# Gated linear attention with an expert layer on one core: a new order of steps, zero products in the head, and the last chunks copied out in halves

## The chip, the cores and the metric

The kernel runs on one core of a Trainium2 chip. The metric is the device time in microseconds (us). The kernel before took 226.56 us as the median of three runs, from 225.03 to 228.58.

## What is computed

```
attention, for each of 4 batches and 8 heads, 768 positions t, head size 48:
    f      = 1 / (1 + exp(-f_logit))
    state  = f[t] * state + outer(k[t], v[t])          # 48 x 48
    y[t]   = q[t] @ state
x = y laid out as 3072 tokens x 384
h = x @ w_in                                            # 384 -> 2048
P = a0 + a1 h + a2 h^2 + a3 h^3
Q = 1 + |b0| |h| + |b1| h^2
out = (P / (Q + 1e-6)) @ w_out                          # 2048 -> 384
```

All inputs and the output are float32; inside, most operands are bfloat16.

## The kernel before

The work is cut into twelve units: unit `n` is one batch and 256 positions (two chunks of 128). Each unit goes through the attention in chunk form and then through the expert layer. The program has no loops over these stages. A string, `ORDER`, lists some 830 steps, each with its unit and its range, and the program emits them in that order. Each engine executes its own steps strictly in the order of the table, and waits at a step until its operands are there, so the table fixes the order on every engine and DMA queue. A trailing `@i` gives the step a new tile in PSUM slot `i`; there are four slots of two banks each, and a new tile waits until the readers of the slot's last tile are done.

The steps of a unit `n`, with the engine in brackets:

- `ld n f|k|q|v`: loads, issued by SP for f, k and q, and by POOL for v (three buffers each). `wi`, `wo`: loads of w_in and w_out in pieces (POOL). `hv 0` is a tiny write that holds w_in's loads back (VectorE). `ab_`, `b1_`: the coefficients.
- `ef`, `ls` (ScalarE): exp of the gates, and log of one plus it. `cs` (TensorE): its cumulative sums. `A n x` (ScalarE): their exponentials. `xa n x` (VectorE): q (x = 0) or k (x = 1) times these.
- `T` (TensorE): transposes; `Te` (VectorE): their copy out of PSUM. `sc`: scores; `mk` (VectorE): scores times mask. `vm`: copies of parts of v (POOL, in unit 0 ScalarE). `sv`, `id` (TensorE): the state's update, `ae` (ScalarE) and `st` (VectorE) its decay. `yb` (TensorE): y; `ye` (ScalarE): its copy out.
- `h n m0 m1` (TensorE): columns m0 to m1 (of 16, each 128 wide) of x @ w_in. `hy` (ScalarE): the copy out; `sa` (ScalarE) or `sq` (VectorE): the square; `ab` (VectorE): the absolute value.
- Q: `u` (TensorE) adds both in PSUM and `ln` (ScalarE) takes the logarithm; or `zd`, an accumulating DMA on POOL's queue, adds them and `lz` (ScalarE) takes the logarithm. `ex` (ScalarE): 1/Q from it.
- P: `p1`, `p2`, `pm` (VectorE), then the sum by `ta` (an accumulating DMA on POOL's queue) or `tv` (VectorE). `gm` (VectorE): P/Q.
- `o n j m0 m1` (TensorE): chunk j's share of the product with w_out. `oe` copies it out (`s` ScalarE, `v` VectorE), `so`, `s0`, `s1` store it (s1 from ScalarE's queue).

In the profile, L200 is a load, L308 `ef`, L313 `ls`, L332 `A`, L337 `xa`, L348 `T`, L356 `Te`, L377 `mk`, L474 `h`, L488 `hy`, L508 `u`, L540 `ex`, L559 `ta`, L525 `zd`, L568 `gm`, L575 `o`, L584 a store, L590 `oe`.

For the last unit, `n` = 11, both chunks' products lie in one tile of one slot (a bank each). The table of before ends with

```
o 11 1 12 16; o 11 0 8 12; oe 11 1 2 v; o 11 0 12 16; s1 11 1 2; s0 11 1 2; oe 11 0 1 s; s1 11 0 1; s0 11 0 1
```

The step `wm` (products of zeros) exists, but the table of before has none.

Of the kernel before, what the change touches and what calls it, by code (L numbers as in the profile page):

```python
# [8 lines left out]
F32 = mybir.dt.float32  # L9
# [10 lines left out]
b1_; cz 3; cb; ld 0 f 2 4; ld 0 f 0 2; ca; cz 0; ld 0 q 2 4; cz 2; ld 0 k 2 4; cz 1; cc; ef 0 2 4  # L20
ld 0 k 0 2; fa 0; ls 0 2 4; ld 0 q 0 2; ef 0 0 2; cs 0 2 4 @0; ls 0 0 2; ld 0 v; A 0 0 2 4
id 0 0 @1; A 0 1 2 4; xa 0 0 2 4; rg; cs 0 0 2 @2; ld 1 f; xa 0 1 2 4; ae 0; A 0 1 0 2; hv 0; ab_
T 0 2 4 @0; wi 0 4; A 0 0 0 2; xa 0 1 0 2; Te 0 2 4; xa 0 0 0 2; sc 0 1 @0; ld 1 k; T 0 0 2 @2
wi 4 8; mk 0 1; vc 0; Te 0 0 2; vm 0 0 s; sv 0; vm 0 1 s; ld 1 v; sc 0 0 @2; st 0 0; ld 1 q; wi 8 16
mk 0 0; id 0 1; st 0 1; yb 0 0 4 @2; ef 1; ld 2 f; fa 1; ls 1; ye 0; cs 1 @1; fb; h 0 0 4 @2; A 1 0
A 1 1; h 0 4 8 @1; hy 0 0 4; xa 1 1; ld 2 k; id 1 0 @2; hy 0 4 8; xa 1 0; ld 2 q; ae 1; sv 1; vm 1 0
vm 1 1; ab 0 0 8; T 1 @1; ld 2 v; sq 0 0 8; Te 1; u 0 0 4 @0; ef 2; ld 3 f; u 0 4 8 @3; st 1 0
ln 0 0 4; p1 0 0 8; id 1 1; sc 1 0 @1; ln 0 4 8; st 1 1; sc 1 1 @0; mk 1 0; ls 2; ex 0 0 8; mk 1 1
id 2 0 @3; ld 3 k; cs 2 @1; pm 0 0 8; yb 1 0 4 @0; A 2 1; wo 8 12; h 0 12 16 @2; p2 0 0 8; ye 1
wo 4 8; xa 2 1; A 2 0; h 1 4 8 @0; wo 0 4; ld 3 q; tv 0 0 8; hy 0 12 16; wo 12 16; h 1 0 4 @1; ae 2  # L30
sa 1 4 8; xa 2 0; ld 4 f; hy 1 4 8; gm 0 0 8; ld 3 v; T 2 @2; hy 1 0 4; vm 2 1; h 0 8 12 @0; Te 2
vm 2 0; sa 1 0 4; sv 2; ab 1 0 8; ef 3; sc 2 0 @1; h 1 12 16 @2; st 2 0; hy 0 8 12; mk 2 0; ls 3
ld 4 k; u 1 0 4 @0; ab 0 8 16; hy 1 12 16; p1 0 8 16; cs 3 @1; ln 1 0 4; sq 0 8 16; h 1 8 12 @2
A 3 0; p2 0 8 16; u 0 12 16 @0; A 3 1; pm 0 8 16; hy 1 8 12; id 2 1; u 0 8 12 @1; ln 0 12 16; st 2 1
sc 2 1 @2; tv 0 8 16; id 3 0 @3; ld 4 q; ln 0 8 12; u 1 4 8 @0; mk 2 1; ae 3; ex 0 8 16
o 0 0 0 4 @1; o 0 0 4 8; p1 1 0 16; yb 2 0 4 @2; ln 1 4 8; o 0 1 0 4; ab 1 8 16; ye 2; xa 3 0
o 0 1 4 8; ex 1 0 8; h 2 0 4 @2; pm 1 0 8; ld 5 f; gm 0 8 16; h 2 4 8 @0; hy 2 0 4; xa 3 1; ef 4
o 0 1 8 12; sq 1 8 16; ld 5 k; o 0 1 12 16; sa 2 4 8; ld 4 v; sv 3; sa 2 0 4; p2 1 0 16; o 0 0 8 12
vm 3 0; ls 4; vm 3 1; ld 5 q; u 1 12 16 @2; st 3 0; ta 1 0 8; hy 2 4 8; pm 1 8 16; o 0 0 12 16
ln 1 12 16; id 3 1; ld 6 f; T 3 @0; st 3 1; ta 1 8 16; ef 5; ab 2 0 8; u 1 8 12 @3; Te 3; oe 0 0 2 s  # L40
zd 2 0 8; h 2 12 16 @2; ln 1 8 12; so 0 0 2; ls 5; sc 3 1 @3; sc 3 0 @0; h 2 8 12 @1; mk 3 1; ld 6 k
ex 1 8 16; ld 5 v; mk 3 0; cs 4 @3; vm 4 1; hy 2 8 12; vm 4 0; cs 5 @0; A 4 0; yb 3 0 4 @1; gm 1 0 8
A 4 1; ye 3; xa 4 0; o 1 0 0 4 @3; hy 2 12 16; o 1 1 0 4; xa 4 1; ld 6 q; h 3 4 8 @1; A 5 0
ab 2 8 16; A 5 1; sq 2 8 16; h 3 0 4 @2; hy 3 4 8; xa 5 0; ef 6; T 4 @0; gm 1 8 16; hy 3 0 4
u 2 12 16 @1; ld 7 f; Te 4; sv 4 @2; ln 2 12 16; id 4 0; ab 3 0 8; sc 4 1 @0; lz 2 0 8; p1 2 0 16
u 2 8 12 @1; o 1 1 4 8; mk 4 1; ln 2 8 12; o 1 1 8 12; o 1 1 12 16; pm 2 8 16; ex 2 0 8; sc 4 0 @1
h 3 12 16 @0; p2 2 0 16; ld 7 k; ae 4; ex 2 8 16; o 1 0 4 8; st 4 0; ta 2 8 16; mk 4 0; id 4 1
o 1 0 8 12; ld 6 v; ld 7 q; o 1 0 12 16; ls 6; xa 5 1; vm 5 0; yb 4 0 4 @1; hy 3 12 16; vm 5 1
st 4 1; pm 2 0 8; ld 8 f; sv 5 @2; oe 1 0 2 s; id 5 0; ef 7; sq 3 0 8; T 5 @3; ta 2 0 8; so 1 0 2
ae 5; ls 7; h 3 8 12 @0; st 5 0; zd 3 0 8; ye 4; Te 5; id 5 1; cs 6 @1; hy 3 8 12; st 5 1  # L50
h 4 4 8 @3; gm 2 8 16; A 6 1; ld 8 k; A 6 0; xa 6 1; h 4 0 4 @0; hy 4 4 8; sq 3 8 16; sc 5 0 @1
sa 4 4 8; h 4 12 16 @2; mk 5 0; hy 4 0 4; ld 8 q; ab 3 8 16; h 4 8 12 @3; vm 6 1; sa 4 0 4; ld 7 v
p1 3 0 16; hy 4 12 16; u 3 12 16 @0; vm 6 0; hy 4 8 12; ab 4 0 8; u 3 8 12 @2; pm 3 8 16; ef 8
sv 6 @3; ln 3 8 12; gm 2 0 8; id 6 0; cs 7 @1; ld 9 f; ae 6; ln 3 12 16; st 6 0; sc 5 1 @2; pm 3 0 8
id 6 1; A 7 1; o 2 0 0 4 @0; ex 3 8 16; o 2 0 4 8; st 6 1; xa 6 0; zd 4 0 8; o 2 0 8 12; o 2 1 0 4
sq 4 8 16; lz 3 0 8; o 2 1 4 8; ab 4 8 16; T 6 @3; mk 5 1; A 7 0; o 2 1 8 12; ld 9 k; o 2 1 12 16
ex 3 0 8; p2 3 0 16; u 4 8 12 @2; xa 7 1; yb 5 0 4 @1; ta 3 0 8; ln 4 8 12; xa 7 0; ta 3 8 16
o 2 0 12 16; ye 5; p1 4 0 16; u 4 12 16 @2; vm 7 1; ld 9 q; ls 8; vm 7 0; h 5 4 8 @1; oe 2 0 2 s
ld 8 v; Te 6; ln 4 12 16; h 5 12 16 @0; pm 4 8 16; sa 5 4 8; so 2 0 2; hy 5 4 8; p2 4 0 16
sc 6 0 @2; cs 8 @3; hy 5 12 16; h 5 0 4 @1; pm 4 0 8; A 8 1; mk 6 0; h 5 8 12 @0; A 8 0; ta 4 0 8  # L60
hy 5 0 4; gm 3 0 8; sc 6 1 @2; sv 7 @3; sa 5 0 4; id 7 0; mk 6 1; ld 10 f; hy 5 8 12; o 3 0 0 4 @1
ta 4 8 16; o 3 1 0 4; gm 3 8 16; ae 7; ef 9; yb 6 0 4 @0; lz 4 0 8; st 7 0; o 3 0 4 8; p1 5 0 16
ld 10 k; o 3 0 8 12; ye 6; ab 5 0 8; o 3 0 12 16; ex 4 8 16; pm 5 0 8; zd 5 0 8; h 6 12 16 @0
xa 8 1; ld 9 v; h 6 8 12 @2; ls 9; ab 5 8 16; vm 8 1; hy 6 12 16; ld 10 q; vm 8 0; sq 5 8 16; id 7 1
o 3 1 4 8; ex 4 0 8; o 3 1 8 12; st 7 1; pm 5 8 16; u 5 8 12 @0; h 6 4 8 @3; hy 6 8 12; p2 5 0 16
ln 5 8 12; h 6 0 4 @2; gm 4 0 8; ta 5 0 8; sa 6 4 8; ab 6 8 16; T 7 @0; hy 6 4 8; ta 5 8 16
gm 4 8 16; o 3 1 12 16; sa 6 0 4; o 4 0 0 4 @3; Te 7; hy 6 0 4; o 4 1 0 4; ld 11 f; ef 10; sq 6 8 16
# [563 lines left out]
```

## Time and profile before

| | us |
|---|---|
| median of three runs | 226.56 (225.03 to 228.58) |
| the profiled execution's own time | 224.93 |
| its span, first to last instruction | 223.2 |
| TensorE busy | 205.2 (92%) |
| VectorE busy | 203.3 (91%) |
| ScalarE busy | 201.1 (90%) |
| GpSimd (POOL) busy | 70.4 (32%) |
| HBM read, written | 25.17 MB, 4.72 MB |

Busy time is what the profiler records between an instruction's start and its end; matmuls overlap, so a busy TensorE isn't one at its peak. A line of the timeline gives start, duration, engine, source line, operation, output and input tiles with their shapes, and in brackets the idle time of the engine before it and what ended that. "PEld" is TensorE's load of weights, "SPq" and "ACTq" are the issues of DMAs by those engines. The chain of work that ended last is followed back from the last instruction, at each step to what released it or to the instruction before it on its engine.

### The profile page before, as it was taken

What the parts mean: (1) busy time and instruction counts of PE and PEld (TensorE: products, weight loads), DVE (VectorE), ACT (ScalarE), POOL (GpSimd) and SP (SyncE); (2) the same over time, 40 slices, a digit from 0 to 9 for tenths busy, and PEclk for the clock granted to TensorE, in tenths of its full rate; (3) what the DMA queues carried; (4) which work ended last, traced back from release to release, by engine and by line L of the source; (5) the groups of instructions that cost most, each with busy time, mean ns of one, the idle gap of its engine ahead of it and who ended that gap; (6) DMA issues with size and microseconds to landing.
All of it is one profiled execution on the core that took longest, in us unless ns stands there. A gap on an engine that the chain in (4) does not pass through costs nothing.

```text
span 223.2 us, 7133 instructions
## 1 busy us (share of the span) xinstructions
PE 205.2 (92%) x3128; PEld 144.0 (65%) x3128; DVE 203.3 (91%) x248; ACT 201.1 (90%) x215; POOL 70.4 (32%) x94
## 2 busy tenths in 40 slices
PE   1786799999999997999999999999999999999991
PEld 1544378566766686567777668678578587785550
DVE  6865999999789997999999999999999999999960
ACT  5645599999999999999999999999999999999960
POOL 3662930021500333107334244041395311341000
PEclk9999999999999999999999999999999999999998
DMA  6999999998999999977999999938869999597434
GB/s 156 225 230 210 237 202 204 193 248 232 170 180 244 243 184 216 260 193 144 171 233 248 209 238 244 213 74 134 171 117 184 207 188 212 112 206 150 94 91 120
DMA packets 61984, 42.33 MB, mean 190 GB/s; under 512 B 51458, under 2 KB 57346, under 8 KB 61954
## 3 DMA queue, kind: packets, MB, share of 16 engines
q0 software_dynamic: 19648, 22.61, 61.6%
q1 hardware_dynamic: 42144, 19.08, 35.0%
q8 instruction: 24, 0.39, 0.6%
q10 hardware_dynamic: 162, 0.20, 0.2%
q14 instruction: 6, 0.05, 0.1%
HBM read 25.17 MB, written 4.72 MB: 134 GB/s over the span
## 4 chain that ended last, share of the span: by engine, by line
PE 62%; ACT 20%; DMA 7%; SPq 4%; issue 3%; DVE 3%
PE op L575 26%; PE hp L474 18%; DMA fn<-in_f_logit_dram 7%; PE u L508 5%; ACT hy L488 4%; PE y L394 4%; ACT lq L516 4%; ACT qi L540 3%; PE tp L348 3%; SPq L200 3%; ACT h L496 3%; ACT A L332 3%; PE sc L369 2%; ACT lsp L313 1%; ACT fn L308 1%
## 5 line engine op out<-in xcount | busy, mean ns | idle before, releaser
L474 PE MATMUL hp<-xT,w_in_sb 128*128 128x256 bf16 x576 | 68.6, 274 | 2.3 <-issue 1.3
L575 PE MATMUL op<-w_out_sb,gall 128*128 128x384 bf16 x384 | 68.7, 326 | 1.1 <-DVE osb L590 0.6
L474 PEld LDWEIGHTS <-w_in_sb 128*128 128x128 bf16 x576 | 55.9, 98 | 12.8 <-issue 3.6
L488 ACT CAST hy<-hp 128x1024 bf16<-128x1024 f32 x48 | 49.5, 1050 | 4.1 <-PE hp L474 4.0
L575 PEld LDWEIGHTS <-gall 128*128 128x128 bf16 x384 | 36.3, 98 | 25.0 <-issue 1.8
L540 ACT ACTIVATE qi<-lq 128x2048 bf16<-128x2048 f32 (+1 forms) x25 | 46.4, 1874 | 0.0
L559 POOL DMA_DIRECT2D gall<-hy x21 | 21.3, 1109 | 64.1 <-PE hp L474 16.4
L377 DVE TENSOR_TENSOR scm<-sc,mask 128x1024 bf16<-128x1024 f32 x24 | 28.7, 1217 | 3.3 <-PE sc L369 3.3
L568 DVE TENSOR_TENSOR gall<-gall,qi 128x2048 bf16<-128x2048 bf16 (+1 forms) x25 | 29.5, 1181 | 0.7 <-ACT qi L540 0.6
L555 DVE TENSOR_TENSOR gall<-gall,h 128x2048 bf16<-128x2048 bf16 (+1 forms) x25 | 29.3, 1177 | 0.0
L388 POOL COPY vmp<-vn 128x128 bf16<-128x128 bf16 x22 | 18.1, 927 | 22.9 <-DMA vn<-in_v_dram 22.9
L525 POOL DMA_DIRECT2D z<-h x12 | 13.2, 1097 | 37.9 <-ACT xT L456 13.4
L516 ACT ACTIVATE lq<-u 128x1024 f32<-128x1024 f32 x24 | 24.5, 1048 | 0.3 <-PE u L508 0.3
L532 ACT ACTIVATE lq<-z 128x2048 f32<-128x2048 bf16 x12 | 23.5, 1956 | 0.0
L492 DVE TENSOR_TENSOR h<-hy 128x2048 bf16<-128x2048 bf16 (+1 forms) x18 | 20.9, 1166 | 0.5 <-ACT hy L488 0.5
L332 ACT ACTIVATE A<-cs 128x768 f32<-128x768 f32 (+1 forms) x26 | 18.9, 786 | 0.7 <-PE cs L323 0.5
L500 DVE TENSOR_SCALAR z<-hy 128x2048 uint16<-128x2048 uint16 (+1 forms) x25 | 16.8, 676 | 1.5 <-ACT hy L488 1.5
L550 DVE TENSOR_SCALAR hy<-hy,a_sb 128x4096 bf16<-128x4096 bf16 (+2 forms) x15 | 16.9, 1128 | 0.1
L545 DVE TENSOR_SCALAR gall<-hy,a_sb 128x4096 bf16<-128x4096 bf16 (+2 forms) x15 | 16.9, 1126 | 0.0
L323 PE MATMUL cs<-lsp,Ui 128*128 128x384 bf16 (+1 forms) x39 | 11.1, 345 | 4.8 <-ACT lsp L313 4.6
L308 ACT ACTIVATE fn<-fn 128x768 f32<-128x768 f32 (+1 forms) x13 | 10.8, 830 | 4.8 <-DMA fn<-in_f_logit_dram 4.8
L356 DVE COPY qkT<-tp 128x2048 bf16<-128x2048 bf16 (+1 forms) x13 | 14.8, 1135 | 0.4 <-PE tp L348 0.4
(69 smaller groups left out, 272.9 us busy)
## 6 DMA issues: line engine op xcount, KB each, us to landing
gall<-hy POOLq DMA_DIRECT2D x21, 512.0 KB, 7.8
z<-h POOLq DMA_DIRECT2D x12, 512.0 KB, 7.3
fn<-in_f_logit_dram SPq DMA_DIRECT2D x11, 384.0 KB, 13.2
kn<-in_k_dram SPq DMA_DIRECT2D x11, 384.0 KB, 11.9
qn<-in_q_dram SPq DMA_DIRECT2D x11, 384.0 KB, 10.6
out_dram<-osb SPq DMA_DIRECT2D x22, 192.0 KB, 4.2
vn<-in_v_dram POOLq DMA_DIRECT2D x11, 192.0 KB, 8.8
w_out_sb<-in_moe_w_out_dram POOLq DMA_DIRECT2D x4, 384.0 KB, 11.6
```

Of the source, the lines that this page charges most:

```text
L332: nc.scalar.activation(t, src, AF.Exp, scale=1.0 if x else -1.0)
L377: nc.vector.tensor_mul(t, s["sc", g].rearrange("s r a i t -> s (r a) (i t)"), mb)
L474: nc.tensor.matmul(t[:, m - m0, :].rearrange("f (j t) -> f j t", j=UB), w_in_sb[:, kk, m * P:(m + 1) * P], s["x"][:, :, kk, :], start=(kk ...
L488: nc.scalar.copy(fl(big(s, "hy", "hy", 3), m0, m1), fl(s["hp", m0], 0, m1 - m0))
L492: nc.vector.tensor_mul(fl(big(s, "h2", "h2", 2), m0, m1), fl(s["hy"], m0, m1), fl(s["hy"], m0, m1))
L516: nc.scalar.activation(fl(s["lq", g], m0 - 8 * g, m1 - 8 * g), fl(s["u", m0], 0, m1 - m0), AF.Ln, scale=rsig2, bias=1.0 + 1e-6)
L532: nc.scalar.activation(fl(s["lq", g], m0 - 8 * g, m1 - 8 * g), fl(s["z"], m0, m1), AF.Ln, scale=rsig2, bias=1.0 + 1e-6)
L540: nc.scalar.activation(fl(s["qi", g], m0 - 8 * g, m1 - 8 * g), fl(s["lq", g], m0 - 8 * g, m1 - 8 * g), AF.Exp, scale=-1.0)
L555: nc.vector.tensor_mul(fl(s["g"], m0, m1), fl(s["g"], m0, m1), fl(s["h2"], m0, m1))
L559: nc.gpsimd.dma_start(out=fl(s["g"], m0, m1), in_=fl(s["hy"], m0, m1), accum_op=ALU.add)
L568: nc.vector.tensor_mul(fl(s["g"], m0, m1), fl(s["g"], m0, m1), fl(s["qi", g], m0 - 8 * g, m1 - 8 * g))
L575: nc.tensor.matmul(s["op"][:, j, 0:DM], s["g"][:, m, C * j:C * j + C], w_out_sb[:, m, :], start=(m == 0), stop=(m == KF - 1))
```

## The change

Three things are changed.

1. `o` gives each chunk of the last unit a PSUM slot of its own. A new step `oc` copies one half (192 columns) of a chunk out; ScalarE takes the first half, VectorE the second.
2. `wm` now multiplies 512 columns of zeros instead of 256, and the table has eight `wm` steps with sixteen products together, all before unit 0's first `h`. `zw` fills the zeros.
3. The table of steps is a new one. It has the same steps in the same sizes, apart from `wm`, `zw` and the last copies, at other places and partly in other PSUM slots. Among what moves: `hv 0` comes before `xa 0 1 2 4`; `T 0 0 2` before `sc 0 1`; `ef 1` and `ls 1` after `ye 0`; `ab_` before `ld 1 f`; `ld 2 v` before `vm 1`; and on ScalarE `ef 3` now follows `hy 0 12 16; hy 0 8 12`.

```diff
 ORDER:
-b1_; cz 3; cb; ld 0 f 2 4; ld 0 f 0 2; ca; cz 0; ld 0 q 2 4; cz 2; ld 0 k 2 4; cz 1; cc; ef 0 2 4
-ld 0 k 0 2; fa 0; ls 0 2 4; ld 0 q 0 2; ef 0 0 2; cs 0 2 4 @0; ls 0 0 2; ld 0 v; A 0 0 2 4
-id 0 0 @1; A 0 1 2 4; xa 0 0 2 4; rg; cs 0 0 2 @2; ld 1 f; xa 0 1 2 4; ae 0; A 0 1 0 2; hv 0; ab_
-T 0 2 4 @0; wi 0 4; A 0 0 0 2; xa 0 1 0 2; Te 0 2 4; xa 0 0 0 2; sc 0 1 @0; ld 1 k; T 0 0 2 @2
...
-id 2 0 @3; ld 3 k; cs 2 @1; pm 0 0 8; yb 1 0 4 @0; A 2 1; wo 8 12; h 0 12 16 @2; p2 0 0 8; ye 1
-wo 4 8; xa 2 1; A 2 0; h 1 4 8 @0; wo 0 4; ld 3 q; tv 0 0 8; hy 0 12 16; wo 12 16; h 1 0 4 @1; ae 2
-sa 1 4 8; xa 2 0; ld 4 f; hy 1 4 8; gm 0 0 8; ld 3 v; T 2 @2; hy 1 0 4; vm 2 1; h 0 8 12 @0; Te 2
-vm 2 0; sa 1 0 4; sv 2; ab 1 0 8; ef 3; sc 2 0 @1; h 1 12 16 @2; st 2 0; hy 0 8 12; mk 2 0; ls 3
...
-ex 11 12 16; o 11 0 4 8; gm 11 8 12; o 11 1 4 8; oe 10 0 2 s; gm 11 12 16; o 11 1 8 12; so 10 0 2
-o 11 1 12 16; o 11 0 8 12; oe 11 1 2 v; o 11 0 12 16; s1 11 1 2; s0 11 1 2; oe 11 0 1 s; s1 11 0 1
+zw; b1_; cz 1; ca; ld 0 f 2 4; ld 0 f 0 2; cz 2; ld 0 q 2 4; cz 0; cb; cz 3; ld 0 k 2 4; cc
+ef 0 2 4; ld 0 k 0 2; fa 0; ls 0 2 4; ld 0 q 0 2; ef 0 0 2; wm 4 @3; cs 0 2 4 @0; ls 0 0 2; ld 0 v
+A 0 0 2 4; id 0 0 @1; rg; xa 0 0 2 4; cs 0 0 2 @2; ab_; ae 0; A 0 1 2 4; hv 0; A 0 1 0 2; wi 0 4
+xa 0 1 2 4; ld 1 f; A 0 0 0 2; xa 0 1 0 2; wm 2 @3; T 0 2 4 @0; xa 0 0 0 2; Te 0 2 4; wm 1 @3
+T 0 0 2 @2; ld 1 k; wi 4 8; ld 1 q; wm 1 @3; sc 0 1 @0; Te 0 0 2; vc 0; mk 0 1; wm 1 @3; sc 0 0 @2
+vm 0 0 s; wm 1 @3; sv 0; vm 0 1 s; mk 0 0; ld 1 v; wi 8 16; st 0 0; fa 1; wm 5 @3; yb 0 0 4 @2; fb
+wm 1 @3; id 0 1; ye 0; ld 2 f; st 0 1; ef 1; h 0 0 4 @2; ls 1; id 1 0 @1; hy 0 0 4; cs 1 @0; ae 1
...
+cs 2 @3; pm 0 0 8; yb 1 0 4 @2; A 2 0; wo 12 16; h 0 12 16 @0; p2 0 0 8; A 2 1; wo 4 8; tv 0 0 8
+ae 2; ye 1; wo 0 4; h 0 8 12 @3; ld 3 q; hy 0 12 16; wo 8 12; xa 2 0; h 1 0 4 @2; hy 0 8 12
+gm 0 0 8; ld 4 f; vm 2 1; ef 3; h 1 4 8 @0; xa 2 1; ld 3 v; sa 1 0 4; ab 0 8 16; vm 2 0; h 1 8 12 @3
+ls 3; p1 0 8 16; hy 1 0 4; sq 0 8 16; sv 2; hy 1 8 12; T 2 @2; st 2 0; p2 0 8 16; sa 1 4 8; id 2 1
...
+tv 11 8 12; o 11 1 0 4 @2; ex 11 12 16; o 11 0 4 8; gm 11 8 12; o 11 1 4 8; oe 10 0 2 s; gm 11 12 16
+o 11 0 8 12; so 10 0 2; o 11 0 12 16; o 11 1 8 12; oc 11 0 0 s; oc 11 0 1 v; o 11 1 12 16; s1 11 0 1
+s0 11 0 1; oc 11 1 0 s; oc 11 1 1 v; s1 11 1 2; s0 11 1 2
 def wm(k, sl):
-        t = slot(sl, [P, 256], F32, "wm")
+        t = slot(sl, [P, 512], F32, "wm")
         for _ in range(k):
-            nc.tensor.matmul(t, zw, _at(zw, [[0, 2], [1, P]]), start=True, stop=True)
+            nc.tensor.matmul(t, zw, _at(zw, [[0, 4], [1, P]]), start=True, stop=True)
 def o(n, j, m0, m1, sl=None):
         s = unit(n)
-        if sl is not None:
-            s["op"] = slot(sl, [P, UB, 512], F32, "op")
+        if sl is not None and n == B * NCC - 1:
+            s["op", j] = slot(sl, [P, 512], F32, "op")
+        elif sl is not None:
+            t = slot(sl, [P, UB, 512], F32, "op")
+            s["op"] = t
+            for i in range(UB):
+                s["op", i] = t[:, i]
         for m in range(m0, m1):
-            nc.tensor.matmul(s["op"][:, j, 0:DM], s["g"][:, m, C * j:C * j + C], w_out_sb[:, m, :],
+            nc.tensor.matmul(s["op", j][:, 0:DM], s["g"][:, m, C * j:C * j + C], w_out_sb[:, m, :],
                              start=(m == 0), stop=(m == KF - 1))
+def oc(n, j, c, eng):
+        s = unit(n)
+        if "osb" not in s:
+            s["osb"] = ms.tile([P, UB, DM], F32, name="osb")
+        cc = slice(c * DM // 2, (c + 1) * DM // 2)
+        (nc.scalar.copy if eng == "s" else nc.vector.tensor_copy)(s["osb"][:, j, cc], s["op", j][:, cc])
```

## The prediction, made before the changed kernel ran

> **What bounds the kernel now.** I read the windows by stage first, then the chain of work that ended last, then the timeline at both ends. Columns of the windows: start:end, length, busy time of PE, PEld, DVE, ACT, POOL, granted clock, DMA share, GB/s.
>
> ```profile
> core 0: us, PE busy (x) PEld busy (x) DVE busy (x) ACT busy (x) POOL busy (x), PEclk, DMA share, GB/s
> 0.00:24.80 24.80, 15.94 (x266) 10.86 (x267) 17.35 (x53) 12.45 (x21) 13.05 (x29) 1.00 1.03 206
> 24.80:62.30 37.50, 35.50 (x559) 24.70 (x557) 35.37 (x39) 37.50 (x43) 10.80 (x16) 1.00 1.16 211
> 62.30:110.00 47.70, 45.82 (x800) 32.64 (x798) 45.87 (x48) 45.99 (x53) 12.79 (x17) 1.00 1.04 203
> 110.00:205.00 95.00, 94.54 (x1445) 68.38 (x1431) 94.00 (x96) 93.87 (x90) 32.96 (x33) 1.00 0.96 189
> ...
> 217.70:223.20 5.50, 0.81 (x4) 0.29 (x3) 0.53 (x1) 0.48 (x1) 0.00 (x0) 0.88 0.44 121
> ```
>
> From 24.8 to 217.7 TensorE, VectorE and ScalarE are all full: ScalarE idles 1.71 + 1.13 = 2.8 us between 62.3 and 205, and not at all before. A new order of the same work has little to win there. What is left is the head (24.8 us, with ScalarE idle for half of it) and the tail (5.5 us). The chain says what ends the head:
>
> ```profile
> 9.59 15.19 DMA fn<-in_f_logit_dram
> 24.80 0.84 ACT fn L308
> ...
> 36.79 0.73 ACT fn L308
> ...
> ACT fn L308 <- DMA fn<-in_f_logit_dram: 3.4, 1, 3.4
> ```
>
> ScalarE stands still for 3.4 us at `ef 2` (exp of unit 2's gates), because that load lands 15.2 us after its issue at 9.59, at 24.78. From there it never rests. The next gate is unit 3's f, in the timeline and in the DMA issues of the window around its issue (last column: us to landing):
>
> ```profile
> 20.45 4.95 SPq L200 DMA_DIRECT2D fn<-in_f_logit_dram  x1
> ...
> fn<-in_f_logit_dram SPq DMA_DIRECT2D x1, 384.0 KB, 15.6
> ...
> 36.65 0.87 ACT L308 ACTIVATE fn<-fn 128x768 f32<-128x768 f32 x1
> ```
>
> It lands at 20.45 + 15.6 = 36.04, and `ef 3` starts at 36.65 without idle time: 0.6 us of room. TensorE's cold start shows in two equal groups of twelve products, and the tail in the last lines of the timeline:
>
> ```profile
> 15.71 2.14 PE L474 MATMUL hp<-xT,w_in_sb 128*128 128x256 bf16 x12
> ...
> 18.78 1.47 PE L474 MATMUL hp<-xT,w_in_sb 128*128 128x256 bf16 x12 [0.93 <-DMA w_in_sb<-in_moe_w_in_dram]
> ...
> 217.67 0.56 DVE L590 COPY osb<-op 128x384 f32<-128x384 f32 x1 [1.81 <-PE op L575]
> ...
> 218.28 0.81 PE L575 MATMUL op<-w_out_sb,gall 128*128 128x384 bf16 x4 [0.65 <-DVE osb L590]
> ...
> 219.13 0.48 ACT L590 COPY osb<-op 128x384 f32<-128x384 f32 x1 [3.31 <-PE op L575]
> 219.63 0.50 ACTq L584 DMA_DIRECT2D out_dram<-osb  x1
> ```
>
> TensorE's last four products wait 0.65 us for VectorE's copy out of the other half of the same PSUM tile.
>
> **What the Trainium skill says.** "TensorE: Matmul & The Clock Gate", Part 1: the array runs at half clock until about 3.4 us of sustained activity. The trace agrees: the twelve products at 15.71 take 2.14 us, those at 18.78 take 1.47, although PEclk stands at 1.00 throughout. "DMA: Bandwidth & Descriptors", Queues, rings and completion order: each DMA engine takes turns between the queues, so what POOL issues slows SP's loads. The trace agrees: DMA share 1.16 between 24.8 and 62.3, and f of unit 3 needs 15.6 us. "PSUM — Partial Sum Buffer", on bank collisions: two engines may not touch one bank at the same time, reads included. So two copies out of one bank have to be ordered; the trace before has no such pair.
>
> **Part 1: sixteen products of zeros (`wm`).** Each has 512 columns; 256 columns take 2.14/12 = 0.18 us cold (a mixed group) and about 0.11 warm, so I estimate 0.43 us cold and 0.22 warm, 3.4 to 6.8 us in all, in TensorE's queue before the first `h`. Four run before 4.64, where TensorE has no work. Two stand ahead of `T 0 2 4` and hold it back about 0.7 us if cold, but its copy (`Te`) now queues behind four `xa` on VectorE (4 x 0.55 us) anyway. Five precede `yb 0`, which waits for `mk 0 0` (end 12.96 before). Added up along VectorE's new order (xa 0.55, Te 0.68, mk 1.2) y of unit 0 starts between 12.2 and 13.0 and ends between 13.2 and 14.4, against 14.5. Then comes the cover: `h 0 0 4` reads the first w_in columns, and their last piece landed at 15.58 (issue 9.21, 6.4 us). The hold on that load (`hv`) moves one `xa` earlier, about 0.4 us. So `h 0 0 4` starts at 15.2 to 15.6, not 15.71, and runs up to 0.6 us shorter. And then nothing: ScalarE meets `ef 2` at the same place of its order and waits for 24.78. Gain taken 0; bounds -0.5 (f of unit 2 lands that much earlier with w_in) and +0.3 (the a and b loads now stand ahead of `ld 1 f` on SP, 1.10 + 0.79 us of issue). If the w_in cover were gone, the zeros would cost up to 1 us.
>
> **Part 2: the new order between 24.8 and 62.** Steps and shapes are the same apart from `wm`, `zw` and the last copies; only positions change. ScalarE's spacing from the timeline: ef 0.75, ln 0.91, ls 0.73, ex 1.80, A 0.69, ae 0.16, ye 0.69, hy 0.90, sa 0.92. Until `ex 0 0 8` ends at 29.89 both orders are the same. Before, ScalarE then does A, ye, A, hy, ae, sa, hy, hy, sa (6.8 us) and meets `ef 3` at 36.65. After, it does A, A, ae, ye, hy, hy (4.0 us) and meets it at 33.92, with the load still 2.1 us away. SP's loads keep their order, and POOL's backlog (w_in, v, w_out) never empties before 43 in either order, so I see no reason for f of unit 3 to come earlier than 36.04. Behind `ef 3` on ScalarE stand `sa 1 0 4`, `ls 3` and `hy 1 0 4`; for `hy 1 0 4` waits `T 2` on TensorE (its PSUM slot), for that `Te 2` on VectorE. ScalarE needs 15.6 us for the rest up to the end of `ex 1 0 8`, before at 50.38: 36.04 + 0.75 + 15.6 = 52.4. **Loss 2.1 us**; bounds 0 (load by 33.9) and +3 (load 0.9 later).
>
> Afterwards all three engines are late by about 2 us. The gaps of ScalarE up to 205 (2.8 us) can take some of it in; I take 0.9, bounds 0 and 2.1.
>
> **Part 3: accumulating DMAs.** `ta` and `zd` add on the DMA queues; landing takes 4.5 to 10.7 us (median 7.8), and no VectorE or ScalarE wait in the trace is put down to one. Counted in ScalarE's work, the old order leaves 13.2 us between `ta 4 0 8` and its reader `gm 4 0 8`, the new one 7.7; VectorE's own work between them is about 6.9 us, and accumulations of 120 to 140 us landed in 8.7. `ta 9 0 8` shrinks from 10.6 to 5.9, `zd 10 0 8` from 7.7 to 5.2, `ta 10 8 16` from 9.9 to 4.5, where landings are 4.5 to 5.9. So `gm 4 0 8` may wait 8.7 - 6.9 = 1.8 us, the late ones up to 1 each, partly in gaps that are there. Taken +1.0, bounds 0 and +3.
>
> **Part 4: the tail.** With a PSUM slot per chunk the 0.65 us wait goes and the last product ends near 217.67 + 0.65 = 218.3, not 219.1: -0.8. But each pair of half copies is in series: in the built program VectorE's copy waits for ScalarE's. 384 columns take 0.48 us on ScalarE and 0.56 on VectorE; 768 take 0.85 on ScalarE, 1 ns a column, so 192 take about 0.30 and, on VectorE, 0.36. With two hops of 0.05 the path from the last product to the store is 0.76 us against 0.54: +0.25. Net **-0.5**, bounds -0.8 (the copies overlap) and -0.1 (ScalarE's earlier store, 0.54 us of issue behind VectorE's first half, holds up its last copy). TensorE stays fed: after the last `u` there are eight groups of 0.65 us = 5.2 us before it needs `gm 11 8 12`, and the chain ln, ln, ex, gm behind it is about 4 us.
>
> **Sum**: 0 + 2.1 - 0.9 + 1.0 - 0.5 = +1.7 us. The profiled execution took 224.93 us (span 223.2 and 1.7 around it), so its like would be 226.6. It lies 1.6 below the median of 226.56; I add the sum to the median: **228.3 us**, 0.8% slower. About 2% (4.5 us) is what a measurement of this kernel can tell from no change, so this counts as within.
>
> **Rivals.**
> *The load isn't late* (0.23): f of unit 3 lands by about 34, or the gaps behind take in the whole wait, and the accumulations land in time. For it: 2.8 us of gaps. Against: VectorE, at 94.00 of 95 us, has hardly any. What remains is head and tail: 226.56 - 0.5 - 0.5 = 225.5.
> *The load is later still* (0.20), the slower side. POOL's v of unit 2 no longer stands behind the two `vm` copies of unit 1, which waited for v until 21.7, so w_out is issued sooner. w_out pieces land about 2.9 us apart; with one more of them ahead, f of unit 3 lands at 38.9, `ef 3` waits 5.0 us and the gaps take in nothing: 226.56 + 5.0 + 1.0 - 0.5 = 232.1. Against: both queues keep their order and were never empty. It decides from a landing at about 38.
> *The head does shrink* (0.07): with f of unit 2 at 21.4 the wait of 3.4 us at `ef 2` goes and the later loads follow: 226.56 - 3.4 - 0.5 - 0.9 = 221.8. Against: total bytes and their order are unchanged.
>
> **Numbers.** Forecast 0.50 (own range 226.3 to 230.8: some two thirds of the way to the joint bounds, which will not all be met together), rivals 0.23, 0.20, 0.07. Range 224.0 to 232.4: it holds the second case and most of the third. Faster by over 2% (below 222.0) is the last case, 0.07; slower (above 231.1) the third and the upper end of the forecast, 0.23; within, 0.70.
>
> **What would show it.** Right: ScalarE idle about 2 us at unit 3's `fn` near 34, released by its DMA; TensorE idle as long before `T 2` near 37 to 39; the first `h` still released by w_in; the 0.65 us before TensorE's last products gone, with a ScalarE and a VectorE copy in series behind them. Wrong: no such wait at `ef 3`; ScalarE at `ef 2` well before 24; a DMA behind VectorE's `gm` for over 2 us.

## The result: 236.1 us, slower by 4.4%

The changed kernel took 236.09 us as the median of four executions (234.89 to 237.08), beside 226.63 for the kernel before in the same set: a ratio of 1.044, with a 95% interval of 1.036 to 1.052. The profiled execution took 236.02 us; its span is 234.3 us, 11.1 more than before. In this document a median is of all executions of a kernel, while a ratio and its interval leave out those that took over 1.5% more than the kernel's fastest. The windows by stage of the changed kernel (columns as for the kernel before; the last line is the tail, 11.1 us later than before):

```profile
core 0: us, PE busy (x) PEld busy (x) DVE busy (x) ACT busy (x) POOL busy (x), PEclk, DMA share, GB/s
0.00:24.80 24.80, 16.78 (x276) 10.43 (x278) 16.53 (x53) 12.25 (x21) 13.79 (x31) 1.00 1.00 198
24.80:62.30 37.50, 29.25 (x432) 20.34 (x432) 28.38 (x31) 28.12 (x32) 5.95 (x9) 0.91 1.06 197
...
110.00:205.00 95.00, 92.94 (x1472) 67.19 (x1474) 93.05 (x93) 92.35 (x92) 33.06 (x33) 1.00 0.92 183
228.80:234.30 5.50, 1.12 (x7) 0.47 (x5) 0.72 (x2) 0.49 (x2) 0.00 (x0) 0.93 0.54 143
```

ScalarE was busy for all of the 37.50 us between 24.8 and 62.3; now it is for 28.12, and TensorE's granted clock is 0.91 instead of 1.00. The waits (total, times, longest) and ScalarE's and TensorE's timelines of the changed kernel say at which instructions:

```profile
ACT fn L309 <- DMA fn<-in_f_logit_dram: 11.2, 3, 5.9
...
PE tp L349 <- ACT hy L489: 4.2, 1, 4.2
...
27.73 0.84 ACT L309 ACTIVATE fn<-fn 128x768 f32<-128x768 f32 x1 [5.87 <-DMA fn<-in_f_logit_dram]
...
42.39 0.84 ACT L309 ACTIVATE fn<-fn 128x768 f32<-128x768 f32 x1 [4.03 <-DMA fn<-in_f_logit_dram]
...
45.83 1.86 PE L349 MATMUL tp<-ident,qkp 128*128 128x128 bf16 x16 [4.22 <-ACT hy L489]
```

The wait is where the prediction put one, at `ef 3`, with `T 2` behind it. But f of unit 3 lands at 42.37, not at 36.04, and f of unit 2 at 27.71, not at 24.78. The losses begin early. The DMA view of the changed kernel between 7.5 and 10 us (first line: busy tenths of the 16 DMA engines in 40 slices of 62 ns), and after it the same view of the kernel before:

```profile
DMA  9998987774433221100000102911223954569578
...
DMA packets 961, 0.26 MB, mean 106 GB/s; under 512 B 961, under 2 KB 961, under 8 KB 961
```

```profile
DMA  9999999999999999999999999899679698994643
...
DMA packets 1587, 0.57 MB, mean 230 GB/s; under 512 B 1529, under 2 KB 1587, under 8 KB 1587
```

In the changed kernel the a and b loads (1.7 us of issue for 3 KB) stand ahead of f of unit 1, which SP issues only at 6.75 instead of 5.08. What was queued before them has moved by about 8; the engines are nearly idle from there to 9.7 us, and 0.31 MB less moves in these 2.5 us. In the kernel before, f of unit 1 fills this time. But a lull follows there too, behind its a and b loads, from about 9.8 to 11 us: between 7.5 and 12.5 us it moves 1.02 MB and the changed kernel 0.88. So this hole is a small part. Experiment 2 shows the larger one, the load of v of unit 2, and experiment 4 that the hole alone does not make f of unit 2 late.

The tail is as predicted. Timeline of the changed kernel:

```profile
229.98 0.32 ACT L605 COPY osb<-op 128x192 f32<-128x192 f32 x1 [1.01 <-PE op L582]
230.34 0.36 DVE L605 COPY osb<-op 128x192 f32<-128x192 f32 x1 [0.97 <-ACT osb L605]
230.73 0.50 ACTq L591 DMA_DIRECT2D out_dram<-osb  x1
```

### The profile page after: what moved, and what is told of

Same layout as the page of the kernel before. It is cut to its first block, busy times and chain, and to the rows that moved or that the text cites. A ratio compares the mean times of both kernels' runs of the same rounds, so it can differ in the third digit from the quotient of the medians.

```text
span 234.3 us, 7140 instructions
## 1 busy us (share of the span) xinstructions
PE 209.4 (89%) x3133; PEld 145.7 (62%) x3144; DVE 205.4 (88%) x250; ACT 202.1 (86%) x216; POOL 72.0 (31%) x94
## 4 chain that ended last, share of the span: by engine, by line
PE 48%; DVE 13%; DMA 11%; ACT 10%; SPq 10%; issue 5%; ACTq 0%; DVEq 0%
PE op L582 18%; PE hp L475 14%; SPq L201 9%; DMA fn<-in_f_logit_dram 8%; PE u L509 5%; PE y L395 3%; DMA gall<-hy 3%; PE tp L349 3%; DVE h L493 2%; ACT hy L489 2%; ACT qi L541 2%; DVE gall L569 2%; PE sc L370 2%; PE cs L324 2%; DVE gall L546 2%
## 5 line engine op out<-in xcount | busy, mean ns | idle before, releaser
L489 ACT CAST hy<-hp 128x1024 bf16<-128x1024 f32 x48 | 48.9, 1040 | 5.6 <-PE hp L475 5.4
L560 POOL DMA_DIRECT2D gall<-hy x21 | 20.6, 1001 | 75.0 <-DVE gall L556 28.4
L389 POOL COPY vmp<-vn 128x128 bf16<-128x128 bf16 x22 | 21.3, 1074 | 27.9 <-DMA vn<-in_v_dram 12.5
L517 ACT ACTIVATE lq<-u 128x1024 f32<-128x1024 f32 x24 | 24.5, 1056 | 1.0 <-PE u L509 1.0
L526 POOL DMA_DIRECT2D z<-h x12 | 14.3, 1193 | 26.8 <-DVE z L501 9.3
L349 PE MATMUL tp<-ident,qkp 128*128 128x128 bf16 x192 | 14.1, 230 | 4.4 <-ACT hy L489 4.2
L338 DVE TENSOR_TENSOR qkp<-qn,A 128x768 bf16<-128x768 f32 (+1 forms) x13 | 11.7, 903 | 6.6 <-DMA qn<-in_q_dram 5.6
## 6 DMA issues: line engine op xcount, KB each, us to landing
w_out_sb<-in_moe_w_out_dram POOLq DMA_DIRECT2D x4, 384.0 KB, 12.5
```

The source lines that it names most:

```text
L389: nc.gpsimd.tensor_copy(dst, src)
L489: nc.scalar.copy(fl(big(s, "hy", "hy", 3), m0, m1), fl(s["hp", m0], 0, m1 - m0))
L517: nc.scalar.activation(fl(s["lq", g], m0 - 8 * g, m1 - 8 * g), fl(s["u", m0], 0, m1 - m0), AF.Ln, scale=rsig2, bias=1.0 + 1e-6)
```

## The experiments

Fourteen kernels ran, one of them twice. Two places in each profiled execution divide its time: where f of unit 3 lands, and where ScalarE is done with `ex 1 0 8` (the start of its next instruction; 50.38 before). What follows to the end of the span is "rest": it is put down to the later table, not to the loads. Each run has one profiled execution, and landings scatter: f of unit 3 lands at 35.17 and at 37.64 in the same program, and at 36.04 and 32.01 in the kernel before and in that of experiment 9, which differ only in the tail. So a difference of a few us between two landings shows little; groups of kernels show more. Times in us.

| kernel | f of units 2, 3 lands | `ex 1 0 8` done | from f3 to it | rest | median |
|---|---|---|---|---|---|
| before | 24.78, 36.04 | 50.38 | 14.34 | 172.85 | 226.6 |
| changed | 27.71, 42.37 | 60.24 | 17.87 | 174.08 | 236.1 |
| a, b back | 25.05, 40.06 | 58.16 | 18.10 | 174.22 | 234.9 |
| v back | 26.57, 37.34 | 53.88 | 16.54 | 173.47 | 230.8 |
| both back | 24.47, 35.17 | 51.71 | 16.54 | 173.21 | 228.9 |
| both back, again | 26.19, 37.64 | 54.17 | 16.53 | 173.52 | 229.9 |
| both back, no zeros | 26.24, 36.05 | 53.28 | 17.23 | 171.70 | 226.7 |
| changed, no zeros | 27.22, 42.51 | 61.49 | 18.98 | 171.79 | 234.5 |
| changed, zeros in gaps | 26.59, 41.27 | 57.81 | 16.54 | 172.29 | 232.8 |

**1. The a and b loads back behind f of unit 1** (`e1_ab_back`)

```diff
-cs 0 0 2 @2; ab_; ae 0; ... xa 0 1 2 4; ld 1 f; A 0 0 0 2
+cs 0 0 2 @2; ae 0; ... xa 0 1 2 4; ld 1 f; ab_; A 0 0 0 2
```

> The changed kernel, with the two tiny loads (`ab_`) moved back behind `ld 1 f` in SP's queue, nothing else. Theory 1 (the tiny loads stop the DMA engines while nothing else is queued, near 8 to 9.7 us): the last piece of the first w_in columns lands near 15.6 again instead of 16.6, f of unit 2 near 25 to 26 instead of 27.7, f of unit 3 near 40 instead of 42.4, and the kernel gains 2 to 3 us. Rival (the earlier hold `hv` and the new order of ScalarE make the loads late, or the zeros): no gain, all landings within 0.5 us of those of the changed kernel.

Measured: 234.88 us (234.09 to 237.6), ratio 1.044 (1.033 to 1.055) to a before of 225.85. That is the ratio of the changed kernel itself, so the gain of 2 to 3 us is missing. The landings are those of theory 1, f of unit 2 2.7 us sooner and f of unit 3 2.3, and `ex 1 0 8` is done 2 us sooner, in one execution. Over all kernels with the new table in which SP issues a and b, f of unit 2 lands at 26.6 to 27.7 with them in front of f of unit 1 (four kernels) and at 24.5 to 26.2 with them behind it (six profiled executions). So their place counts for 1 to 2 us of that landing here; no gain in time is shown for this move alone.

**2. The load of v of unit 2 back behind unit 1's `vm`** (`e2_v_back`)

```diff
-sv 1; ld 2 v; ab 0 0 8; ... vm 1 1; st 1 0
+sv 1; ab 0 0 8; ... vm 1 1; ld 2 v; st 1 0
```

> The changed kernel, with `ld 2 v` moved back behind the two `vm` copies of unit 1 on POOL, nothing else. Theory 2 (before, POOL's queue ran empty near 25 to 27 us, since v of unit 2 was issued only at 23.4, and SP's loads then ran alone at some 300 GB/s; in the changed kernel v closes that gap): f of unit 2 stays at 27.7, but q of unit 2 and f of unit 3 land 2 to 4 us sooner (f of unit 3 at 38 to 40), and the kernel gains 2 to 4 us. Rival (SP's loads are late only by what they lost before 10 us): f of unit 3 at 42.4 still, no gain.

Measured: 230.79 us, ratio 1.025 (1.016 to 1.034). f of unit 3 lands at 37.34, five us sooner, and the interval is clear of the changed kernel's (1.036 to 1.052). In the changed kernel v of unit 2 was issued at 18.02 instead of 23.35, into the time when f, k and q of unit 2 should have come: q of unit 2 landed at 37.71, against 28.43 before. The queues between 24.8 and 27.5 us (packets, MB, share of the engines' time), in the kernel before and then in the changed one:

```profile
q1 hardware_dynamic: 1416, 0.53, 73.9%
q0 software_dynamic: 542, 0.16, 54.8%
```

```profile
q0 software_dynamic: 841, 0.20, 73.7%
q1 hardware_dynamic: 839, 0.32, 67.0%
```

Before, POOL's queue (q0) has little to send there, and SP's (q1) moves 0.53 MB; in the changed kernel v of unit 2 is in POOL's queue and SP's moves 0.32; with v back it moves 0.76. In the five kernels with v early f of unit 3 lands at 39.1 to 42.5, in all others at 37.6 or sooner. This is the largest single part of the loss.

**3. Both back** (`e3_both_back`, and the same program once more, `e3b_both_back`)

> Both of these in one kernel; everything else as changed. If the two theories are the whole of the head's loss, f of unit 2 lands near 24.8 and f of unit 3 near 36, `ef 3` still waits about 2 us, and the kernel takes what the prediction's sum gave, 228 +- 1.5 us against 226.6 before. If the ScalarE order, the zeros or the rest of the new table cost more than that sum says, it stays at 230 or more.

> The changed kernel with both moves of loads undone and the zeros in place, once more, beside the kernels of this set, since its four executions ran from 226.6 to 230.6. If the zeros cost something by the clock: a median of 228.5 or more and a mean granted clock about 0.985. If not: 226.5 to 227.3, as without zeros.

Measured: 228.9 us (226.6 to 230.6), ratio 1.016 (1.007 to 1.025); the second time 229.92 (226.0 to 234.0, too wide for a ratio). f of unit 3 lands at 35.17 and 37.64, about where the prediction took it (36.04). The medians are 3.1 and 3.5 us above those of the kernel before in their sets, where the prediction's sum was 1.7. What is left over is of the size of what the zeros cost (experiment 6).

**4. Both early loads in the kernel before** (`b3_both_in_before`)

```diff
-ld 1 f; xa 0 1 2 4; ae 0; A 0 1 0 2; hv 0; ab_
+ab_; ld 1 f; xa 0 1 2 4; ae 0; A 0 1 0 2; hv 0
-sv 1; vm 1 0; vm 1 1; ab 0 0 8; T 1 @1; ld 2 v; sq 0 0 8
+sv 1; ld 2 v; vm 1 0; vm 1 1; ab 0 0 8; T 1 @1; sq 0 0 8
```

> The kernel before, with only the two moves of the change made in it: `ab_` ahead of `ld 1 f`, and `ld 2 v` ahead of unit 1's `vm`. Theories 1 and 2: f of unit 2 lands near 27.7 and f of unit 3 near 41 to 42; `ef 2` waits 6 us; since `ef 3` stands later on ScalarE, the loss is smaller than the change's: 4 to 7 us, about 231 to 234 us. Rival: no loss over 1 us.

Measured: 228.94 us over 20 executions, ratio 1.012 (1.009 to 1.015): a loss of 3 us, less than the 7 between the changed kernel and both back. f of unit 3 lands at 39.08, but ScalarE's longest wait for `fn` is 2.3 us, and `ex 1 0 8` is done 13.72 after the landing. The old order has 2.8 us more of ScalarE's work ahead of `ef 3` to fill the wait. The same late load costs more in the new table.

Theory 1 fails here: f of unit 2 lands at 22.75, two us sooner than in the kernel before and not three later, though the hole is the same (0.33 MB between 7.5 and 10 us). By 12.5 us the bytes are made up: 1.01 MB since 7.5. What else differs from the changed kernel is w_in: its first load is issued at 7.33 here and at 6.79 there, where its hold `hv 0` stands one `xa` earlier, and between 10 and 12.5 us SP's queue moves 0.59 MB here and 0.44 there. So it may take the hole and the earlier w_in together to make f of unit 2 late. No run moves `hv 0` alone, and this stays open.

**5. `ef 3` and `ls 3` later** (`e5_ef3_later`, both loads back)

```diff
-vm 2 1; ef 3; h 1 4 8 @0; ... ls 3; p1 0 8 16; ... sa 1 4 8; id 2 1
+vm 2 1; h 1 4 8 @0; ... p1 0 8 16; ... sa 1 4 8; ef 3; ls 3; id 2 1
```

> The changed kernel with both moves of loads undone (the a and b loads behind f of unit 1, v of unit 2 behind the copies of unit 1's v), and beside that exp and log of unit 3's gates (ef 3, ls 3) moved later on ScalarE, behind the square sa 1 4 8: four steps of ScalarE, about 3.6 us, now stand ahead of the wait. Without this move the kernel took 228.9 us, 3.0 more than before, with f of unit 3 landing at 35.2 and a wait of up to 3.8 us for it. Theory A (the place of ef 3 costs what the prediction gave it, 2.1 us): 226.6 to 227.2, and no wait for f of unit 3 over 0.5 us. Rival B (the wait is slack that the gaps behind it take in, the loss is in the later table: accumulations, copies): 228.5 or more. Rival C (what waits behind ef 3 on ScalarE is not what is late; cs 3 or the rest of unit 3 is): slower than 229.

Measured: 229.86 us, ratio 1.019 (1.014 to 1.024), no gain. f of unit 3 landed at 36.38 and `ex 1 0 8` was done 17.91 us later, where the place of the change gives 16.54. Its rivals B and C came. The 2.1 us cannot be had by moving these two steps; it seems that what is behind them in the table expects them early.

**6. Without the zeros** (`e6_no_zeros`, both loads back; `x2_after_no_zeros`, the changed kernel): the eight `wm` steps are taken out.

> The changed kernel with both moves of loads undone, and without the eight steps of zero products. Theory A (the zeros are hidden behind w_in's landing and warm nothing that counts): 228.5 to 229.3, equal to the 228.9 with them, the first h still released by w_in. Rival B (they cost): 228.0 or less. Rival C (they pay, as the products of the head run cold without them): 229.7 or more; the first twelve products of h then take about 2.1 us again and not 1.5.

> The changed kernel without its eight steps of zero products, the loads left where the change put them. Without zeros the kernel with both loads moved back took 226.7 us and with them 228.9, though the profiled executions of the two were equal (226.7 and 226.6). Theory A (zeros make the head's products end sooner, so TensorE stands idle longer before unit 1 and 2 and its clock is halved once more in many executions): 234 or less, the mean granted clock higher than with zeros. Rival B (the difference of 2.2 us was chance, four executions against 22): 235.5 to 236.5.

Measured: 226.74 us over 22 executions, ratio 1.006 (1.004 to 1.009), against 229 to 230 with them; and 234.54, ratio 1.035 (1.029 to 1.041), against 236.1. By the medians the zeros cost 2 to 3 us and about 1.5, where I had costed them at nothing. In each case the interval overlaps that of the kernel with zeros a little, so neither shows it alone. Theory A's clock is not the cause in the changed kernel: its mean is 0.978 without zeros and 0.976 with them. The first twelve products of `h` take 2.72 us without and 1.47 with them, but the time comes from elsewhere: the table's "rest" is 171.7 and 171.8 without them, and 173.2 to 174.2 with the sixteen products alone. TensorE's waits in the changed kernel that have no releaser, and one of them in its timeline:

```profile
PE y L395 <- issue: 1.8, 1, 1.8
PE op L582 <- issue: 0.7, 1, 0.7
...
141.22 0.25 PE L395 MATMUL y<-scm,vn 64*32 64x128 bf16 x4
143.28 0.24 PE L395 MATMUL y<-scm,vn 64*32 64x128 bf16 x4 [1.81 <-issue]
```

It stops in the middle of eight products that belong together, with nothing to wait for. The two kernels without zeros show no such wait of 0.5 us or more (a third, the last of experiment 10, has one of 0.7), both back with zeros 0.9 and 1.4. Taking all such waits of 0.4 us or more off, the rest is 171.5 to 172.8 in all eleven profiled executions of the new table, with zeros and without. Around the wait shown (138.5 to 143.5) the DMA view of the changed kernel has a packet of TensorE's instructions:

```profile
q8 instruction: 1, 0.02, 1.2%
```

The Trainium skill ("Runtime: NRT & Kernel Launch", Instruction fetch mechanics) says that instructions come in blocks of 16 KB, 256 of them, by DMA and that this is mostly hidden. Here q8 brings 24 such packets (0.39 MB), and it isn't always hidden. In the seventeen profiled executions there are 21 such waits of 0.4 us or more behind the first 15 us. Counted over TensorE's matmuls and weight loads they all stand at one place modulo 256: at 179 to 181 where the trace has all records, at 171 to 175 in the five that lack 11 to 15 of them. Each time TensorE goes on 1.2 to 1.6 us after a packet on q8 has ended. The zeros' 32 instructions (a product and its weight load each) shift which work falls at the end of a block. That the fetch is the cause is argued from this; no run took it away alone.

**7. Zeros in the two gaps** (`x1_zeros_in_gaps`, the changed kernel)

```diff
 def add(n, j, sl=None):      # id
         nc.tensor.matmul(s["sv"][:, j], ident, s["st"][j], ...)
+        if n == 2 and j == 0: wz(2, 40)
-hy 1 8 12; T 2 @2
+hy 1 8 12; wz 2 66; T 2 @2
+def wz(n, k):
+        for _ in range(k):
+            nc.tensor.matmul(unit(n)["svt"][:, 1, 384:512], zw, zw, ...)
```

> The changed kernel with zero products added in the two long gaps of TensorE that the late loads leave: 40 of 128 columns (2.2 us) where unit 2's sums wait for ls 2 behind ef 2 (idle 28.8 to 31.2), and 66 (3.7 us) ahead of T 2, which waits behind ef 3 (idle 41.6 to 45.8). They go to a spare part of a PSUM tile that is live there. The question is what the granted clock of 0.50 after these gaps (32 to 35.5 and 46 to 49.5) costs. Theory A (TensorE's half clock after an idle stretch is a second loss on top of the late loads): the clock stays at 1.00 in both places and the time falls by 2 to 3.5 us, to 232.6 to 234.1 from 236.1; the mean granted clock rises from about 0.975 to 0.99 or more. Rival B (ScalarE and VectorE set the pace there and a slow TensorE is hidden): the clock rises, the time stays within 1 us of 236.1. Rival C (zeros don't hold the clock): no change of either.

Measured: 232.81 us (231.1 to 234.4), ratio 1.030 (1.025 to 1.036). The windows around the gaps, of the changed kernel and then of this one:

```profile
32.00:35.00 3.00, 3.00 (x85) 2.08 (x84) 0.63 (x1) 3.00 (x5) 1.56 (x2) 0.52 1.25 204
...
46.00:49.00 3.00, 2.78 (x19) 2.08 (x19) 0.95 (x2) 2.52 (x3) 0.00 (x0) 0.50 0.91 218
```

```profile
32.00:35.00 3.00, 3.00 (x33) 2.69 (x29) 0.00 (x0) 3.00 (x6) 0.87 (x1) 1.00 1.24 204
...
46.00:49.00 3.00, 2.92 (x30) 1.46 (x29) 3.00 (x4) 3.00 (x4) 0.00 (x0) 1.00 0.90 224
```

The clock is 0.50 for some 3.5 us after each gap in the changed kernel and 1.00 with zeros in it; the transposes of `T 2` take 1.05 us, not 1.86. The Trainium skill ("TensorE: Matmul & The Clock Gate", HAM oscillation) warns of just this, idle gaps of over about 3.4 us. The trace agrees for the gap of 4.2 us, but shorter ones do it here too: 2.4 us behind one of 1.3, and in both back 1.0 behind one of 1.3 (clock 0.50 from 30 to 32). Its price is in the table: with the full clock from the landing on, f of unit 3 is followed by `ex 1 0 8` after 16.53 to 16.54 us in four executions of the list above, and with a halved clock behind the gap (changed, a and b back, changed without zeros) after 17.87, 18.10 and 18.98. Holding the clock took 17.87 to 16.54, so 1.3 us; the other two would be 1.6 and 2.4, if the clock is all of it there. (In both back without zeros, with 17.23, ScalarE comes to `ef 3` only 0.7 us after the landing, so it is no case of a wait, and I leave it out.) The rest of the gain here has other causes: f of unit 3 landed 1.1 sooner, and this execution shows no wait for "issue" (rest 172.29 against 174.08).

**8. Zeros in the gap with both loads back** (`y1_both_back_gap_zeros`)

```diff
+        if n == 2 and j == 0: wz(2, 16)
```

> The changed kernel with both moves of loads undone and its zeros in place (229.4 and 229.9 in two sets, mean clock about 0.985), with 16 more zero products of 128 columns (0.9 us) where unit 2's sums wait for ls 2 (idle 27.0 to 28.0, and longer in other executions). Theory A (what the zeros of the head cost there, 2 to 3 us against the same kernel without them, is a half-clock window more after this gap): the clock rises to 0.992 or more and the time falls to 226.5 to 227.5. Rival B (the zeros cost by something else): less than 1 us of gain, 228.5 or more.

Measured: 232.48 us, ratio 1.025 (1.020 to 1.031), in the medians slower by 3 than without them (228.9 and 229.92; the 229.4 above is a slip): the rival's cause, but dearer than it said. Before 53 us nothing is lost (16.53 from landing to `ex 1 0 8`); the rest is 178.0, with these waits of TensorE:

```profile
PE y L402 <- issue: 2.7, 1, 2.7
PE op L592 <- issue: 2.6, 2, 1.5
```

Together 5.3 us, and the clock is halved after the longest. This speaks for the count of instructions as what zeros cost.

**9. The tail alone, in the kernel before** (`b4_tail_in_before`)

```diff
-o 11 1 0 4
+o 11 1 0 4 @1
-oe 11 1 2 v; o 11 0 12 16; s1 11 1 2; s0 11 1 2; oe 11 0 1 s
+oc 11 1 0 s; oc 11 1 1 v; o 11 0 12 16; s1 11 1 2; s0 11 1 2; oc 11 0 0 s; oc 11 0 1 v
```

> The kernel before, with the tail of the changed kernel alone: a PSUM slot for each chunk of the last unit, and each chunk copied out in two halves by ScalarE and VectorE. The prediction's term: -0.5 us (bounds -0.8 and -0.1), so 225.3 to 225.4 beside 225.85; the wait of 0.65 us of TensorE's last four products gone, and 0.75 us from the last product to the store's issue where it was 0.54. Rival: the wait is gone, but the halves in series and the stores that stand behind one another give it back: no change within 0.2.

Measured: 226.02 us beside 225.93, ratio 1.003 (1.000 to 1.006). In its profile the last store is issued at 219.10, against 219.63 before: the 0.5 us is there in this one execution, but it is less than the medians can tell.

**10. Four kernels meant to be faster than both.** The a and b loads go to ScalarE's queue, ahead of `A 0 0 2 4`: alone in the kernel before (`v2_ab_act_in_before`), with a slot for each of the last chunks and whole copies (`v1_ab_act_slots`), with 12 zero products more (`v4_slots_ab_few_zeros`), and in the new table without zeros and with v back (`y2_new_table_ab_act`).

```diff
 def load_ab():
-        nc.sync.dma_start(...)        # both loads
+        nc.scalar.dma_start(...)
```

> A try at beating both: the kernel before, with the a and b loads issued early from ScalarE's queue, not in SP's queue between the loads of the units, and with a PSUM slot for each of the last chunks but whole copies as before (VectorE one chunk, ScalarE the other). If the tiny loads leave a hole in SP's queue in the kernel before too (9.5 to 11 us), f of unit 2 lands 1 to 1.5 us sooner, the wait of 3.4 us at ef 2 shrinks by as much, and the tail gives another 0.65: 223.5 to 224.5. If the tiny packets cost the engines their time wherever they stand, only the tail is left: 225.2. If their issues (two of about 0.5 us) delay ScalarE's exponentials of unit 0, up to 1 us slower than that.

> The kernel before with the a and b loads on ScalarE's queue, and nothing else changed (the tail with one slot for both of the last chunks and its wait of 0.65 us). With the slots as well it took 224.6 beside 225.9. If the loads give the gain and the tail nothing, as the tail alone gave nothing in the kernel before: 224.4 to 224.8. If the slots with whole copies give their 0.65: 225.2 to 225.5.

> A second try at beating both: the kernel before with the a and b loads on ScalarE's queue and a slot for each of the last chunks (224.6 us), and 12 zero products of 128 columns (0.67 us) where unit 2's sums wait for ls 2. A third of that kernel's executions had a mean clock of 0.992 or less and took 225.4 to 226.6, the others, at 0.997 to 1.000, 223.8 to 225.1. If the clock falls because of that gap, the slow third goes and the median is 224.2 to 224.5; if it falls elsewhere, the median stays at 224.6, and if the gap is shorter than the zeros they cost up to 0.5.

> The changed kernel without zeros, with v of unit 2 behind the copies of unit 1's v, and with the a and b loads on ScalarE's queue instead of SP's. With the a and b loads in SP's queue behind f of unit 1 it took 226.7. In the kernel before, the same move and a slot for each of the last chunks gave 1.3 us together. Theory A (the tiny loads leave a hole in SP's queue in either place): f of unit 2 lands about 1 us sooner than at 26.2, and the time is 225.3 to 225.9. Rival (the new table doesn't use an earlier f of unit 2, since f of unit 3 is what it waits for): 226.4 or more.

Measured: 224.58 us with slots, ratio 0.997 (0.994 to 1.000); 225.96 without, 0.998 (0.995 to 1.001); 228.16 with the 12 zeros, 1.011 (1.005 to 1.016); 225.10 in the new table, 0.997 (0.994 to 1.000). In the profiled executions f of unit 2 lands at 21.3 to 22.8 and f of unit 3 at 31.0 to 31.6 in all four (24.78 and 36.04 in the kernel before; 23.93 and 32.01 with the tail alone), and next to nothing comes of it in the kernel before: `ex 1 0 8` is done at 50.3 to 51.9, where it was 50.38. Once a load is in time, a sooner one is worth nothing. In the new table `ex 1 0 8` is done at 50.98: with f of unit 3 there before ScalarE comes to `ef 3`, the new order loses nothing, as the lower bound of part 2 had it (load by 33.9). The kernel with slots is the fastest of all, by 0.3% at most, at the edge of what was measured. The 12 zeros, which were to cost 0.5 at most, cost some 3 us, and here the intervals (1.005 to 1.016, 0.994 to 1.000) are apart. TensorE's wait for nothing at this place is 2.91 us, 1.51 without them, and its clock is 0.72 between 86 and 90:

```profile
86.53 3.94 PE L484 MATMUL hp<-xT,w_in_sb 128*128 128x256 bf16 x23 [2.91 <-issue]
```

## Why the prediction was wrong

The prediction was 228.3 us (224.0 to 232.4); 236.1 is outside. Step by step, with the profiled executions:

- **Part 2, `ef 3` (+2.1): the step that failed is the landing it starts from.** I left f of unit 3 at 36.04 because "SP's loads keep their order, and POOL's backlog (w_in, v, w_out) never empties before 43 in either order", and looked for a reason for an earlier landing, not for a later one. The backlog does run low in the kernel before: between 24.8 and 27.5 SP's queue moves 0.53 MB beside POOL's 0.16. The early v of unit 2 takes that time away, and SP's queue moves 0.32. The landing was 42.37, 6.3 later; with v put back alone it was 37.34. ScalarE stood idle for 4.0 us to 42.4 and TensorE for 4.2 ahead of `T 2`, where I had about 2 near 34 and 37 to 39.
- **Part 2, behind the landing: the mechanism is right, and a term is missing.** I reckoned 0.75 + 15.6 = 16.35 from the landing to the end of `ex 1 0 8`; with the full clock it is 16.54, against 14.34 before, so the order costs 2.2, about what I said. What was missing is the halved clock behind the gap, 1.3 more. Landing 6.33, order 2.20 and clock 1.33 make 9.86 of the span's 11.1, and `ex 1 0 8` is done at 60.24, 9.86 after 50.38. Where f of unit 3 lands as assumed and there are no zeros (both back without zeros, 36.05), the ratio of 1.006 (1.004 to 1.009) is a loss of 1.4 us, against the sum's 1.7.
- **Part 1, the head (gain 0, bounds -0.5 and +0.3): missed too, by less.** The first `h` was still released by w_in, but at 16.77, not at 15.2 to 15.6, and f of unit 2 landed 2.9 us later. The a and b loads ahead of `ld 1 f` were priced at their issue (1.9 us of SP), and not at what the DMA engines have queued meanwhile; how much is theirs and how much is that of the earlier hold on w_in is not separated. And the zeros, costed at nothing beside the work that covers them, cost 1.5 to 3 us by the medians, a hundred us later and more: it seems by their 32 instructions in TensorE's stream.
- **Parts 2, 3 and 4 together behind that (-0.9 + 1.0 - 0.5 = -0.4): not contradicted.** The rest is 171.79 in the changed kernel without zeros against 172.85 before, 1.1 less; but that is the length of a wait for nothing which TensorE has in the kernel before (1.14 us at 85.56), so nothing is left beyond the scatter. With zeros it is 174.08: 2.3 more, about what TensorE's two waits for nothing (1.8 + 0.7) make. An accumulating DMA holds VectorE's `gall` for 0.9 us in the changed kernel, of the size expected. The single terms were not measured apart.
- **The tail (-0.5): right**, the 0.65 us wait is gone, the two copies are in series as the timeline above shows, and the last store is issued 0.53 sooner in the one profiled execution where it was tried alone; the medians don't show it.
- **The rival "the load is later still" was what happened**, and its mechanism was named: v of unit 2 no longer stands behind the two `vm` copies. I gave it 0.20 and sized it by one w_out piece more ahead of f of unit 3 (38.9). Its point of decision, a landing at about 38, was met; but it is the early v itself that takes the time, from f, k and q of unit 2 and not only from f of unit 3, and w_out is issued only 1.0 us sooner. What I held against it, that both queues "were never empty", was wrong for POOL's queue near 26 us, and in the changed kernel for SP's between 8 and 10.

## What to carry to other kernels

When a table of steps is changed, follow each DMA queue past each moved step, and ask what the DMA engines have queued at that moment, on both queues: a load issued earlier takes its time from those that were in flight on the other queue. Where one queue runs low, the other makes up lost time, and a load moved into such a lull takes that away. Look for late landings as hard as for early ones, since a late landing is paid at the wait and again in TensorE's clock behind the gap, while an early one is worth nothing once the wait is gone. Filler work on TensorE was not free here though it was hidden where it stood.

## What was unexpected of the hardware

- Two queues in use share the engines about packet by packet: between 17 and 30 us in the changed kernel q0 (POOL) moves 1.43 MB in 2851 packets and q1 (SP) 1.23 MB in 3250; q1's packets are small (0.38 KB), so beside POOL it gets about 95 KB/us, and between 7.5 and 9 us in the kernel before, nearly alone, close to 300. What SP doesn't move while it is alone it moves at a third of the speed. A second queue of small packets also lowers the sum: with v in the lull between 24.8 and 27.5 us (q0's packets there are 0.24 KB on average) both queues together move 193 GB/s, and 264 before.

```profile
q0 software_dynamic: 2851, 1.43, 78.9%
q1 hardware_dynamic: 3250, 1.23, 50.8%
```

- TensorE can stand still for 0.5 to 2.9 us with nothing to wait for, in straight code, at one place in each block of 256 instructions at most and 1.2 to 1.6 us behind a packet of instructions. With 24 to 32 instructions more or less, over 50 us earlier, such waits come, grow or go: 1.14 us in the kernel before, 1.51 with the two loads moved and slots, 2.91 with 12 zero products more.
